# A linear-attention and SoLU feed-forward kernel: h multiplied by its exponential inside PSUM, three passes reading it there, two small negations on ScalarE, and a new order list

## The chip, the cores and the metric

The kernel runs on one core of a Trainium2 chip. The metric is the device time of one execution in microseconds (us). TensorE (PE) multiplies matrices, with a sequencer that also loads weights (PEld). VectorE (DVE), ScalarE (ACT) and GpSimd (POOL) do elementwise work, and SyncE (SP) issues the DMAs. Matrix products land in PSUM, which DVE and ACT can read and write here; everything else lives in SBUF.

## The reference

Inputs are q, k and v of shape 8 x 8 x 576 x 64 (batch, heads, sequence, head dimension), a weight of 512 x 1024, a weight of 1024 x 512 and a gain of 1024.

```python
q_s = softmax(q over the head dimension)          # exp(q - max) / (sum + 1e-9)
k_s = softmax(k over the sequence)
kv  = einsum('bhsd,bhse->bhde', k_s, v)
x   = einsum('bhsd,bhde->bhse', q_s, kv)          # then laid out as 4608 x 512
h   = x @ w_in                                    # 4608 x 1024
sm  = exp(h - max(h)) / (sum + 1e-9)              # per row
solu = h * sm
mu, var = mean and variance of solu per row
ln  = (solu - mu) / sqrt(var + 1e-6) * g_ln
out = ln @ w_out                                  # 4608 x 512
```

## The kernel before, in words

The 4608 rows are cut into 36 row tiles of 128 rows: four per batch, named b_c (batch 0 to 7, piece 0 to 3), and one more for each pair of batches that holds the last 64 rows of both (1_4, 3_4, 5_4, 7_4). The weights arrive as 64-bit floats in pairs of 32-bit words. They are rebuilt as 32-bit floats (lines 238 to 244; tiles iw and gw), scaled, and split into a high and a low fp16 part (lines 269, 271, 310 and 312; tiles wi and wo). Every matrix product of the feed-forward part is the sum of three fp16 products: high by high, high by low, low by high.

Each batch first has its keys (K) and queries (Q) put through the softmax: differences, exponentials, sums and products over 128 x 1024 pieces (lines 347 to 365 and 414 to 432), on DVE, ACT and POOL. For a row tile, `attend` (x) gives x transposed in two fp16 parts (xT, lines 505 and 507). `hidden` (h) does the following:

- 24 matmuls of 512 columns (line 522) into a PSUM tile h of 128 x 1024 fp32 (two of the 2-KB banks). There are two such tiles (tag "h", bufs=2), so the h of one tile has to wait until the tile two places earlier has let its buffer go.
- the negated row maximum (`top`, DVE, line 529), and `nm`, that times a scale (line 531).
- the exponential of h into an SBUF tile e, with its row sum (ACT, line 535).
- a chain of numbers per row, am, pi, p and ph (lines 539 to 548, POOL or DVE), which turns the maximum into a safe scale.
- s1: h times ph times e, written over e in SBUF, with its row sum (DVE, line 551). This is the last pass that reads h. Then `nmu`, the negated mean (line 553).
- u: the high fp16 part of e + nmu (ACT, line 556) and the low part (DVE, line 558); a DMA transposes both into uT (line 561). There are twelve uT buffers, so the h of many tiles can run ahead of their o.
- s2: the sum of squares of e + nmu (ACT, line 565), and another chain of numbers to r (POOL or DVE, lines 569 to 578).

`project` (o) multiplies uT by wo in 24 steps (line 593), into the only PSUM tile of tag "o", scales it by a number per row (line 601 on DVE or 603 on ACT) and stores it.

Each engine runs its instructions strictly in the order in which the program issues them. That order is written by hand: ORDER is a list of names; each name runs one more step of that piece of work (h5, o3, K2, Q2a, V21 and so on), up to its next `yield`. The letters after a dot (.v) put a step on DVE that would go to POOL or ACT. P is a step of four warm-up matmuls of TensorE, LK, LQ, LV, LG are loads, W and Z scale the two weights, w and y are the rebuilding of them.

Of the kernel before, what the change touches and what calls it, by code (L numbers as in the profile page):

```python
# [8 lines left out]
F32 = mybir.dt.float32  # L9
# [75 lines left out]
)  # L85


@with_exitstack
def linear_attention_solu_ffn(ctx: ExitStack, tc: tile.TileContext, q, k, v, w_in, w_out, g_ln, out):

# [420 lines left out]
    def hidden(row_tile):  # L511
# [50 lines left out]
        uT_of[row_tile] = uT  # L562
        yield
        s2 = sm.tile([P, 1], F32, name=f"s2{name}", tag="s2")
        nc.scalar.activation(e, e, AF.Square, bias=nmu, accum_out=s2)  # L565
        yield

        z1 = sm.tile([P, 1], F32, name=f"z1{name}", tag="z1")
# [144 lines left out]
```

## Time and profile before

| quantity | us |
|---|---|
| median of three runs | 516.03 |
| lowest and highest run | 513.93, 517.16 |
| the profiled execution | 514.96 |
| its span, first to last instruction | 513.1 |
| PE busy | 461.9 |
| DVE busy | 400.3 |
| ACT busy | 261.8 |
| POOL busy | 237.2 |

An engine's busy time is the time in which at least one of its instructions ran. Matmuls overlap one another, so a PE that is busy is not a PE at its peak. The profiled execution is 1.9 us longer than its span, and 1.1 us below the median of the runs.

### The profile page before, as it was taken

To read this page: it belongs to the slowest core of one execution; us is meant where nothing else is said; L and a number is where in the kernel's file an instruction comes from. 1 tells how busy PE (TensorE), PEld (TensorE's weight loads), DVE (VectorE), ACT (ScalarE), POOL (GpSimd) and SP (SyncE) were. 2 spreads that over 40 slices of the span, in tenths; PEclk is the share of its full clock that TensorE was granted. 3 is DMA by queue.
4 is the path that set the end of the run, shared out by engine and by line. 5 is a ranking of instruction groups with operands and counts; after the bars stand their busy time and mean duration, and the time that the engine had idled before them with its cause. 6 is when DMAs were issued, how large, how long until landed. Compare 5 with 4: busy or idle time off the path is not lost.

```text
span 513.1 us, 7978 instructions
## 1 busy us (share of the span) xinstructions
PE 461.9 (90%) x2986; PEld 234.5 (46%) x2986; DVE 400.3 (78%) x674; ACT 261.8 (51%) x378; POOL 237.2 (46%) x316
## 2 busy tenths in 40 slices
PE   4075796899989999999999999999999999999986
PEld 1043443444455444555554545544554544444434
DVE  4999999999989998989878896968876443455431
ACT  2466557876563644674446656444556423533430
POOL 5424686553884762937464367432552221202320
PEclk9578887999999999999999999999999999999999
DMA  7789649683778699758944866966072542252251
GB/s 268 204 243 257 144 135 205 158 163 98 118 186 202 154 182 221 143 101 231 210 98 118 222 134 158 203 173 131 14 144 64 122 77 69 61 125 61 61 144 41
DMA packets 159238, 74.97 MB, mean 146 GB/s; under 512 B 127840, under 2 KB 152672, under 8 KB 159200
## 3 DMA queue, kind: packets, MB, share of 16 engines
q1 hardware_dynamic: 159200, 74.47, 62.8%
q8 instruction: 23, 0.38, 0.3%
q14 instruction: 15, 0.12, 0.1%
HBM read 36.70 MB, written 9.44 MB: 90 GB/s over the span
## 4 chain that ended last, share of the span: by engine, by line
PE 44%; DVE 38%; POOL 5%; DMA 4%; issue 4%; ACT 3%; SPq 1%; DVEq 0%; POOLq 0%; ACTq 0%
PE o L593 22%; PE h L522 18%; DVE e L551 3%; DVE top L529 3%; DVE u L558 3%; DVE qsum L421 3%; DVE vm L150 2%; DMA w_in<-in_moe_w_in_dram 2%; DVE khalf L347 2%; DVE wi L271 1%; DMA qm<-in_q_dram 1%; DVE qnmx L414 1%; PE kv L375 1%; DVE wo L312 1%; POOL km L358 1%
## 5 line engine op out<-in xcount | busy, mean ns | idle before, releaser
L522 PE MATMUL h<-wi,xT 128*128 128x512 f16 x864 | 204.9, 384 | 7.4 <-DVE e L551 4.9
L593 PE MATMUL o<-wo,uT 128*128 128x512 f16 (+1 forms) x888 | 199.2, 373 | 3.8 <-DVE os L601 3.2
L593 PEld LDWEIGHTS <-uT 128*128 128x128 f16 x888 | 86.0, 98 | 99.9 <-issue 5.2
L522 PEld LDWEIGHTS <-xT 128*128 128x128 f16 x864 | 83.5, 99 | 105.5 <-issue 6.1
L529 DVE TENSOR_REDUCE top<-h 128x1 f32<-128x1024 f32 x36 | 43.8, 1216 | 38.7 <-PE h L522 38.6
L535 ACT ACTIVATE e<-h,nm,hs 128x1024 f32<-128x1024 f32 x32 | 38.4, 1201 | 49.8 <-DVE nm L531 38.5
L556 ACT ACTIVATE u<-e,nmu 128x1024 f16<-128x1024 f32 x36 | 41.1, 1146 | 38.3 <-DVE nmu L553 38.2
L558 DVE SCALAR_TENSOR_TENSOR u<-e,nmu,u 128x1024 f16<-128x1024 f32 x36 | 53.6, 1490 | 8.3 <-ACT u L556 8.2
L551 DVE SCALAR_TENSOR_TENSOR e<-h,ph,e 128x1024 f32<-128x1024 f32 x36 | 45.9, 1274 | 4.5 <-POOL ph L548 3.5
L539 POOL TENSOR_SCALAR am<-nm 128x1 f32<-128x1 f32 x22 | 12.7, 577 | 77.7 <-DVE nm L531 66.0
L565 ACT ACTIVATE e<-e,nmu 128x1024 f32<-128x1024 f32 x36 | 41.1, 1142 | 14.3 <-DVE u L558 14.3
L416 POOL TENSOR_TENSOR qm<-qm,qnmx 128x1024 f32<-128x1024 f32 (+1 forms) x13 | 26.6, 2050 | 29.0 <-DVE qnmx L414 29.0
L545 POOL TENSOR_TENSOR p<-pi,mone 128x1 f32<-128x1 f32 x36 | 21.6, 599 | 35.1 <-DVE pi L542 33.7
L427 POOL TENSOR_TENSOR qm<-qm,qrec 128x1024 f32<-128x1024 f32 (+1 forms) x13 | 26.7, 2056 | 20.0 <-DVE qrec L425 15.5
L432 POOL TENSOR_TENSOR qhl<-qm,qhl 128x1024 f16<-128x1024 f32 (+1 forms) x12 | 25.9, 2162 | 16.8 <-ACT qhl L148 12.5
L505 ACT ACTIVATE xT<-x 128x512 f16<-128x512 f32 x36 | 20.8, 589 | 24.1 <-PE h L522 14.3
L603 ACT ACTIVATE os<-o,rr 128x512 f32<-128x512 f32 x23 | 15.7, 683 | 29.5 <-PE o L593 15.7
L375 PE MATMUL kv<-vm,km 128*64 128x65 f32 x512 | 22.1, 228 | 8.3 <-ACT vm L148 4.9
L418 ACT ACTIVATE qm<-qm 128x1024 f32<-128x1024 f32 (+1 forms) x17 | 16.9, 1000 | 22.1 <-POOL qm L416 15.9
L358 POOL TENSOR_TENSOR km<-km,kb 128x1024 f32<-128x1024 f32 x9 | 23.3, 2585 | 8.6 <-ACT kb L333 8.3
L507 DVE SCALAR_TENSOR_TENSOR xT<-x,xT 128x512 f16<-128x512 f32 x36 | 24.3, 681 | 3.4 <-ACT xT L505 3.3
L578 POOL TENSOR_TENSOR r<-var,mhalf 128x1 f32<-128x1 f32 x36 | 24.6, 684 | 4.8 <-DVE var L575 3.7
(136 smaller groups left out, 658.6 us busy)
## 6 DMA issues: line engine op xcount, KB each, us to landing
v<-in_v_dram SPq DMA_DIRECT2D x32, 256.0 KB, 3.6
out_dram<-os SPq DMA_DIRECT2D x31, 256.0 KB, 3.2
qm<-in_q_dram SPq DMA_DIRECT2D x7, 1024.0 KB, 6.4
km<-in_k_dram SPq DMA_DIRECT2D x7, 1024.0 KB, 6.3
w_in<-in_moe_w_in_dram SPq DMA_DIRECT2D x8, 512.0 KB, 6.9
w_out<-in_moe_w_out_dram SPq DMA_DIRECT2D x8, 512.0 KB, 5.5
out_dram<-os SPq DMA_DIRECT2D x10, 128.0 KB, 2.6
qm<-in_q_dram SPq DMA_DIRECT2D x2, 512.0 KB, 4.3
```

What stands on the lines that cost most here:

```text
L358: on(nc.gpsimd).tensor_tensor(km[:, hs], km[:, hs], wide, op=ALU.subtract)
L375: nc.tensor.matmul(o, km[:, h + i, c], vm[:, h + i, c], start=(c == 0), stop=False)
L416: on(nc.gpsimd).tensor_tensor(x, x, wide(nmx), op=ALU.add)
L427: on(nc.gpsimd).tensor_tensor(x, x, wide(rec), op=ALU.mult)
L522: nc.tensor.matmul(h[:, ns], xT[:, t, kc], wi[:, s, kc, ns], start=(i == 0), stop=(i == len(terms) - 1))
L529: nc.vector.tensor_reduce(top, h, axis=AX.X, op=ALU.max, negate=True)
L535: nc.scalar.activation(e, h, AF.Exp, bias=nm, scale=hs, accum_out=z)
L551: nc.vector.scalar_tensor_tensor(e, h, ph, e, op0=ALU.mult, op1=ALU.mult, accum_out=s1)
L556: nc.scalar.activation(u[:, 0], e, AF.Identity, bias=nmu)
L558: nc.vector.scalar_tensor_tensor(u[:, 1], e, nmu, u[:, 0], op0=ALU.add, op1=ALU.subtract)
L565: nc.scalar.activation(e, e, AF.Square, bias=nmu, accum_out=s2)
L593: nc.tensor.matmul(o, uT[:, j, f], wo[:, s, f, cols], start=(f == 0 and j == 0 and s == 0), stop=(f == NF - 1 and j == 1))
```

## The change: what it does, and the diff

1. s1 (line 551) writes its product over h in PSUM and no longer over e in SBUF. The three passes behind it read it from h: u high (line 556, ACT), u low (line 558, DVE) and s2 (line 565, ACT). s2 leaves its unused squares in e. In the program as built, the first matmul into an h buffer now waits for ACT (for s2 of the tile two places earlier), where before it waited for DVE (for s1). s2 still stands behind u low, as before.
2. nm (line 531) and nmu (line 553), 36 of each, go from DVE to ACT.
3. The warm-up matmuls write into the PSUM tile of tag "o" (bufs=1) and no longer into that of tag "h".
4. ORDER is another list. DVE has 578 rows and had 635; ACT has 374 and had 293. Apart from nm and nmu, some steps change engine. DVE has 12 of the key differences (line 358) for 7, 7 of the query differences (line 416) for 4, and 6 of the query products (line 427) for 4. It has 9 of the copies of v (line 150) for 14. POOL has 4 key differences for 9, 10 query differences for 13 and 11 query products for 13.

```diff
 ORDER = (
-    "LQ0*2 w0 Q0a Q0a.v LK0 w0 Q0b Q0a*2 Q0c w0 K0 w1 Q0a LK0 w0 Q0a K0 Q0b*2 w0*2 w1 V02 w2 Q0c Q0b "
...
+    "LK0*3 w3 K0*2 w3 V00 LQ0 K0*3 P*4 K0*3 LQ0 w0*2 K0 w3 V00 K0.v LV0 w3 K0 w3 K0.v w3 K0*2 Q0a Q0b w0 "
...
 )
@@ hidden
         nm = sm.tile([P, 1], F32, name=f"nm{name}", tag="nm")
-        nc.vector.tensor_scalar(nm, top, hs, None, op0=ALU.mult)
+        nc.scalar.activation(nm, top, AF.Copy, scale=hs)
...
-        nc.vector.scalar_tensor_tensor(e, h, ph, e, op0=ALU.mult, op1=ALU.mult, accum_out=s1)
+        nc.vector.scalar_tensor_tensor(h, h, ph, e, op0=ALU.mult, op1=ALU.mult, accum_out=s1)
         nmu = sm.tile([P, 1], F32, name=f"nmu{name}", tag="nmu")
-        nc.vector.tensor_scalar(nmu, s1, -1.0 / DF, None, op0=ALU.mult)
+        nc.scalar.activation(nmu, s1, AF.Copy, scale=-1.0 / DF)
...
-        nc.scalar.activation(u[:, 0], e, AF.Identity, bias=nmu)
-        yield
-        nc.vector.scalar_tensor_tensor(u[:, 1], e, nmu, u[:, 0], op0=ALU.add, op1=ALU.subtract)
+        nc.scalar.activation(u[:, 0], h, AF.Identity, bias=nmu)
+        yield
+        nc.vector.scalar_tensor_tensor(u[:, 1], h, nmu, u[:, 0], op0=ALU.add, op1=ALU.subtract)
...
-        nc.scalar.activation(e, e, AF.Square, bias=nmu, accum_out=s2)
+        nc.scalar.activation(e, h, AF.Square, bias=nmu, accum_out=s2)
@@ warm_up
-            acc = ps.tile([P, DF], F32, name=f"warm_up{len(warmed)}", tag="h", bufs=2)[:, 0:DM]
+            acc = ps.tile([P, DM], F32, name=f"warm_up{len(warmed)}", tag="o", bufs=1)
```

The first place is DVE in the first row tiles. In the kernel before, from s1 of tile 0_1 on (L529 is top, L551 s1, L558 u low, the gw rows rebuild the second weight):

```order
L551 SCALAR_TENSOR_TENSOR e0_1_534,s10_1_569<-h0_1_462,ph0_1_553,e0_1_534 128x1024
L553 TENSOR_SCALAR nmu0_1_571<-s10_1_569 128x1
L244 SCALAR_TENSOR_TENSOR gw0_524<-w_out0_313,gw0_524 128x1024
L242 SCALAR_TENSOR_TENSOR gw3_530<-w_out3_374,gw3_530 128x1024
L529 TENSOR_REDUCE top0_0_597<-h0_0_511 128x1
L531 TENSOR_SCALAR nm0_0_599<-top0_0_597,hs0_484 128x1
L244 SCALAR_TENSOR_TENSOR gw3_530<-w_out3_374,gw3_530 128x1024
L558 SCALAR_TENSOR_TENSOR u0_1_609<-e0_1_534,nmu0_1_571,u0_1_609 128x1024
L529 TENSOR_REDUCE top0_3_684<-h0_3_585 128x1
```

And in the changed kernel, from s1 of its first tile, 0_0, on:

```order
L551 SCALAR_TENSOR_TENSOR h0_0_408,s10_0_535<-h0_0_408,ph0_0_529,e0_0_481 128x1024
L507 SCALAR_TENSOR_TENSOR xT0_2_525<-x0_2_468,xT0_2_525 128x512
L358 TENSOR_TENSOR km1_299<-km1_299,kb1_533 128x1024
L558 SCALAR_TENSOR_TENSOR u0_0_542<-h0_0_408,nmu0_0_537,u0_0_542 128x1024
L242 SCALAR_TENSOR_TENSOR gw0_441<-w_out0_380,gw0_441 128x1024
L244 SCALAR_TENSOR_TENSOR gw0_441<-w_out0_380,gw0_441 128x1024
L529 TENSOR_REDUCE top0_1_586<-h0_1_449 128x1
```

Between s1 and u low there were six instructions, the top of the next tile among them; now there are two, and the next top stands behind u low.

The second place is ACT in the same tiles. In the kernel before, from u high of tile 0_1 on (L535 is the exponential, L556 u high, L565 s2):

```order
L556 ACTIVATE u0_1_609<-e0_1_534,nmu0_1_571 128x1024
L148 COPY vm_76<-v1_3_550 128x8x64
L360 ACTIVATE km1_350<-km1_350 128x1024
L535 ACTIVATE e0_0_626,z0_0_627<-h0_0_511,nm0_0_599,hs0_484 128x1024
L148 COPY vm_76<-v1_2_582 128x8x64
L238 ACTIVATE gw1_654<-w_out1_602 128x1024
L565 ACTIVATE e0_1_534,s20_1_688<-e0_1_534,nmu0_1_571 128x1024
```

In the changed kernel, from nm of tile 0_0 on:

```order
L531 ACTIVATE nm0_0_461<-top0_0_459,hs0_439 128x1
L535 ACTIVATE e0_0_481,z0_0_482<-h0_0_408,nm0_0_461,hs0_439 128x1024
L148 COPY vm_76<-v1_1_484 128x8x64
L505 ACTIVATE xT0_2_525<-x0_2_468 128x512
L333 COPY kb1_533<-wide1_520 128x512
L553 ACTIVATE nmu0_0_537<-s10_0_535 128x1
L505 ACTIVATE xT0_3_540<-x0_3_500 128x512
L556 ACTIVATE u0_0_542<-h0_0_408,nmu0_0_537 128x1024
L565 ACTIVATE e0_0_481,s20_0_567<-h0_0_408,nmu0_0_537 128x1024
```

s2 stood five instructions behind u high, with the exponential of the next tile between them; now it follows at once, and nm and nmu stand in ACT's row.

## Rows read from the trace of the kernel before

**Rows 1.** The page: busy time of each engine, and the span in 40 slices

```profile
PE 461.9 (90%) x2986; PEld 234.5 (46%) x2986; DVE 400.3 (78%) x674; ACT 261.8 (51%) x378; POOL 237.2 (46%) x316
PE   4075796899989999999999999999999999999986
DVE  4999999999989998989878896968876443455431
```

**Rows 2.** Stretches: us, busy (instructions) of each engine, PEclk, DMA share, GB/s

```profile
0.00:51.00 51.00, 22.33 (x145) 11.00 (x146) 41.88 (x63) 25.54 (x35) 21.66 (x19) 0.76 0.86 242
51.00:130.00 79.00, 69.79 (x446) 35.38 (x444) 77.13 (x117) 53.10 (x78) 47.30 (x57) 0.92 0.65 149
130.00:215.00 85.00, 79.69 (x556) 41.70 (x555) 79.84 (x128) 45.34 (x67) 54.83 (x58) 1.00 0.84 177
215.00:270.00 55.00, 54.21 (x446) 29.22 (x444) 48.01 (x87) 28.74 (x43) 30.29 (x39) 1.00 0.70 160
270.00:488.00 218.00, 217.36 (x1297) 107.01 (x1296) 147.34 (x272) 105.58 (x155) 80.17 (x136) 1.00 0.50 113
488.00:513.00 25.00, 18.49 (x107) 10.18 (x105) 6.14 (x11) 3.51 (x5) 2.98 (x9) 1.00 0.38 95
```

**Rows 3.** Groups by form: busy us, mean ns | idle before, who ended it

```profile
L558 DVE SCALAR_TENSOR_TENSOR u<-e,nmu,u 128x1024 f16<-128x1024 f32 x36 | 53.6, 1490 | 8.3 <-ACT u L556 8.2
L551 DVE SCALAR_TENSOR_TENSOR e<-h,ph,e 128x1024 f32<-128x1024 f32 x36 | 45.9, 1274 | 4.5 <-POOL ph L548 3.5 <-ACT e L535 0.2
L529 DVE TENSOR_REDUCE top<-h 128x1 f32<-128x1024 f32 x36 | 43.8, 1216 | 38.7 <-PE h L522 38.6
L556 ACT ACTIVATE u<-e,nmu 128x1024 f16<-128x1024 f32 x36 | 41.1, 1146 | 38.3 <-DVE nmu L553 38.2
L565 ACT ACTIVATE e<-e,nmu 128x1024 f32<-128x1024 f32 x36 | 41.1, 1142 | 14.3 <-DVE u L558 14.3
L507 DVE SCALAR_TENSOR_TENSOR xT<-x,xT 128x512 f16<-128x512 f32 x36 | 24.3, 681 | 3.4 <-ACT xT L505 3.3
L531 DVE TENSOR_SCALAR nm<-top,hs 128x1 f32<-128x1 f32 x32 | 6.9, 214 | 1.2
L553 DVE TENSOR_SCALAR nmu<-s 128x1 f32<-128x1 f32 x36 | 5.5, 153 | 1.3
```

**Rows 4.** Single lines: duration in ns, lowest/median/highest, first and last start

```profile
L558 DVE SCALAR_TENSOR_TENSOR u<-e,nmu,u x36: 1264/1281/3142, 77.8 to 493.9; 128x1024 f16<-128x1024 f32 x36
L551 DVE SCALAR_TENSOR_TENSOR e<-h,ph,e x36: 1192/1276/1286, 68.4 to 491.2; 128x1024 f32<-128x1024 f32 x36
L271 DVE SCALAR_TENSOR_TENSOR wi<-iw,s_in,wi x4: 1191/2012/2322, 47.0 to 57.0; 128x1024 f16<-128x1024 f32 x4
```

**Rows 5.** Instructions in order of time: start us, us; ACT at the start

```profile
2.01 0.20 ACT L137 ACTIVATE warm<-mhalf 128x1 f32<-128x1 f32 x1
```

**Rows 6.** Instructions in order of time, the last two row tiles

```profile
478.63 1.22 DVE L529 TENSOR_REDUCE top<-h 128x1 f32<-128x1024 f32 x1 [4.99 <-PE h L522]
...
481.55 1.28 DVE L551 SCALAR_TENSOR_TENSOR e<-h,ph,e 128x1024 f32<-128x1024 f32 x1 [0.19 <-ACT e L535]
...
491.20 1.28 DVE L551 SCALAR_TENSOR_TENSOR e<-h,ph,e 128x1024 f32<-128x1024 f32 x1
...
493.90 1.28 DVE L558 SCALAR_TENSOR_TENSOR u<-e,nmu,u 128x1024 f16<-128x1024 f32 x1 [1.22 <-ACT u L556]
...
495.22 1.15 ACT L565 ACTIVATE e<-e,nmu 128x1024 f32<-128x1024 f32 x1 [1.35 <-DVE u L558]
```

**Rows 7.** The chain of waits, pieces in order of time: start us, us, what

```profile
119.79 1.15 DVE top L529
...
126.03 1.29 DVE e L551 x2
...
306.87 5.18 PE o L593 x24
...
312.48 0.06 PE x L471
```

124 rows, old and new, of the table ORDER are left out of this document.

## The prediction

> **What bounds the kernel now.** I read the page first [rows 1]. PE is the busiest engine, but its row is full only from the middle of the span on, while DVE's row is full from the second slice to about the fifteenth. The stretches say it more exactly [rows 2]. From 51 to 130 us DVE runs 77.1 of 79 us and PE 69.8; from 270 to 488 us PE runs 217.4 of 218 and DVE only 147.3. So the first part is DVE's and the second PE's. In the first part the two are coupled: every h needs DVE passes, and PE's work behind any point cannot begin before they end.
>
> The useful sum is therefore: when DVE has done what one h buffer waits for, plus the PE work that stands behind that h in program order. PE takes 0.216 us for a step of 512 columns (24 steps in 5.18 us) and 0.06 for a small step of attention [rows 7]. For DVE I went through its order list and gave each instruction the lowest or typical undisturbed duration of its line, less 0.07 us, since the next one starts that much before the end of the one ahead: a top of 1.22 moves the chain on by 1.15 [rows 3, 7].
>
> First point, in the kernel before: the h of tile 1_4 waits for s1 of 1_2. DVE's undisturbed work up to there is 95.1 us. It ended at 127.3 (126.03 + 1.28) [rows 7, 4]. Idle time explains 11.0 of the difference (51 - 41.9 and 79 - 77.1) [rows 2]. The other 21.2 us are DVE passes that lasted longer than they must. The lines show who suffers: u low takes 1.26 to 3.14 us, wi 1.19 to 2.32; both read two tensors from SBUF. s1, which reads one of its two from PSUM, never takes over 1.29 [rows 4]. POOL has 19 large passes (lines 358 to 432) ahead of that point, so a POOL pass costs DVE 1.12 us.
>
> Behind the point PE has 672 steps of h and 822 of o, 322.7 us, and 41.1 of small matmuls: 363.8. Sum 491.1. The span is 513.1; the 22 us between are PE's later gaps (5.3 us from 130 to 215, 6.5 in the last stretch [rows 2]), further disturbed passes and the drain.
>
> **The change part by part.** nm and nmu leave DVE: 32 and 4 times 0.214 plus 36 times 0.153 are 13.2 us [rows 3]. ACT takes 72 instructions; the nearest row is its 128x1 activation of 0.20 us [rows 5], so 14.4 us on an engine busy for half the span [rows 1]. The chain of a tile keeps its length (0.20 for 0.21 and 0.15) unless ACT is just in a pass of some 1.1 us [rows 3], so 0 to 1.1 us for each of 72; I take 0.2, and DVE's other work ahead of s1 hides it in the early tiles.
>
> In return DVE gets work from POOL: 5 more key differences, 3 query differences and 2 query products of about 1.2 us each undisturbed, 12 us. Against that stand five copies of v fewer and some small numbers per row. DVE's total is about even; what counts is the work ahead of the two points below.
>
> u low reads one tensor from SBUF. If it then behaves as s1 and xT do, its mean of 1490 ns falls to about 1270 [rows 3, 4]: 8 us of DVE over 36 tiles, 2.2 of it in the first ten. u high and s2 from PSUM: u high and s2 last 1146 and 1142 from SBUF, and I take the same, as ACT has room.
>
> s1 writes to PSUM. No row shows DVE writing there. Below, it costs nothing new: 1274 ns, as now with its read from PSUM [rows 3]. Above, if reading and writing one bank took turns, every element would pay twice, and s1 would grow by (1274 - 681) / 512 x 1024 = 1.19 us. I take the lower end, since s1 and u low differ by 5 ns in the median although one reads PSUM and the other does not [rows 4].
>
> The h buffer is held longer. Before, s1 frees it; now s2 does. From the end of the matmuls to the end of s2 the shortest chain of the trace is 2.92 (top to s1) plus 5.17 (s1 to s2), 8.1 us [rows 6], where it was 4.2. **Here a rule speaks against the change.** The rows show that a pass from PSUM costs DVE no more than one from SBUF (1276 against 1281 ns) [rows 4], so only the hold can cost. The Trainium skill, PSUM — Partial Sum Buffer, Summary: rules for kernel authors, says to evacuate promptly because PSUM is tight, and its page VectorE: DVE Perf Modes, Rules for kernel authors, would copy h out first if many operations follow. By the first rule the sum would rise as the second rival below does; by the rows the copy of the second would save nothing per pass.
>
> The order list answers to the hold. Between the last h step of a tile and the first of the tile two later, PE now has 7.7 to 9.2 us of other work in the first three tiles, and 13 to 21 in most that follow; before it was mostly 6 to 15. Only three later places are under 10 (9.6, 7.8, 9.1). What the buffer allows is thus mostly covered by the o steps that are put between.
>
> Now the same sum for the changed kernel. First point: h of 1_0 waits for s2 of 0_3. DVE's undisturbed work up to u low of 0_3 is 85.6, idle as before 11.0, POOL has 11 large passes ahead, 12.3; s2 ends 1.2 after u low [rows 6]. That is 110.1. Behind it PE has 744 steps of h and 816 of o, 337.0, and 43.7 of small ones: 380.7. Sum 490.8, against 491.1: DVE is 17 us earlier, but PE has 17 us more left.
>
> Second point, the largest later sum of each. Before: h of 3_1 waits for s1 of 2_3, 148.3 + 11.0 + 34 POOL passes x 1.12 (38.1) = 197.4, and 298.2 behind: 495.6. After: h of 2_2 waits for s2 of 2_1, 151.1 + 11.0 + 24 x 1.12 (26.9) + 1.2 = 190.2, and 305.8 behind: 496.0. From this 2.2 come off for u low. To be added are DVE's waits inside a tile: s1 cannot start before 1.7 us after top, nor u low before 1.4 after s1 [rows 6]. DVE's new order leaves less than that between them in few early tiles: 0.4 us missing up to this point, 3.8 over fourteen tiles, where the old order missed 0.2. I add 1. So 494.8 against 495.6.
>
> Between these points the old kernel's sums lie within some 6 us of its largest from tile 0_2 to 4_3; the new one's lie 5 to 10 below their largest at most tiles behind 3_1. A flat line of near-ties adds more small waits, and I take 1 more off. The later stretch has the same PE work and PE is full there [rows 2]. The missing waits of DVE over all tiles, 24 us, fall mostly there, where DVE idles for 71 us. The warm-up matmuls and the four more of them cost nothing: PE waits for weights then.
>
> Total -2 us: 514.96 - 2 = 513.0. The profiled execution lies 1.1 below the median of the runs, so by medians it is -0.6%.
>
> **The rivals.** (1) Faster: POOL's passes stop hurting. Two-input passes of DVE meet fewer and shorter POOL passes, and u low, the worst sufferer, leaves that group. If a POOL pass costs DVE half of 1.12, the 24 passes ahead of the second point give back 13 us there (to 481.8), the 11 ahead of the first 6 (to 484.8). The larger of the two then sets the end, 10 lower, and the time is 503. For it: 21 us of the first 127 are such loss. Against it: the steps that moved to DVE, key and query differences, read two tensors from SBUF themselves. Beside it the Trainium skill, SBUF — State Buffer, Who interferes with whom, says that a DVE operation with two SBUF inputs and a GpSimd operation that reads SBUF block each other for the whole instruction; by that rule u low can no longer be blocked, which the 3.14 against 1.29 us of the rows supports.
>
> (2) Slower: the hold. Where PE's cover is under 12 us, in eleven of 34 places, DVE's in-order list and ACT's queue stretch the 8.1 us to 10 to 13. If PE waits 1 us in each, the time is 524, and this decides from the point at which the hold exceeds the cover in more than about five places at 1 us. For it: the shortest covers, 7.7 to 9.2, are no longer than the shortest hold. Against it: in the early tiles this wait is the one already counted in the sums.
>
> (3) Slower: s1's write into PSUM costs the 1.19 us. Ten or eleven s1 stand ahead of the second point: 12 to 13 us more, 526.
>
> (4) The change does not do what it says: the passes from PSUM and nm on ACT are in the order lists, so this can only mean that contention and hold both do nothing. That is the forecast.
>
> **How the numbers follow.** A measurement of this kernel can tell about 1%, 5.2 us, from no change: faster means below 510.9 and slower above 521.2. Forecast 0.42, rival 1 0.34, rival 2 0.17, rival 3 0.07. The range reaches past rival 1's 503 to 501 and to the upper rivals' 526; beyond it lie some 0.12 of rival 1 and 0.08 of rivals 2 and 3, as each of these spreads by several us. The likeliest case's own range is 509 to 519, by the spread of the two points' sums and the waits added. Faster 0.34, same 0.42, slower 0.24.
>
> **What would show it.** In the changed profile: u low near 1.27 us and never over 1.3; s1 near 1.28 (rival 3 if near 2.4); nm and nmu near 0.2 on ACT. The first stretch to 130 us should have DVE as full as now, and PE's idle time before h should name ACT (s2); over 8 us of it in all would be rival 2. DVE's two-input passes in the first 130 us show rival 1: the sum of what they last beyond their lowest, 21 us now, should be 12 at the first point, under 7 for rival 1. A first top earlier or later than now by over 4 us, from the new order of the loads, would upset the idle 11 us that I kept, and with it the whole sum one for one.

## The result, and the profile after

The changed kernel takes 510.97 us (median of five runs, 509.67 to 511.37), the kernel before 514.36 in the same rounds (513.93 to 517.16). The ratio is 0.9916 with a 95% interval of 0.9891 to 0.9941: 0.8% faster. Forecast were 513.0 and -0.6%. The span fell from 513.1 to 509.2 us.

Of the page, the busy times and two of the rows in 40 slices, which answer to [rows 1]:

```profile
PE 463.3 (91%) x2990; PEld 235.3 (46%) x2990; DVE 374.5 (74%) x618; ACT 279.7 (55%) x457; POOL 197.5 (39%) x293
PE   7357875999999999899999999999999999999986
DVE  3999999999898989778867777788765464342521
```

DVE and POOL have 26 and 40 us less to do, ACT 18 more. DVE is still full up to the fifteenth slice or so, and PE behind it. The stretches, with the columns of [rows 2]:

```profile
0.00:51.00 51.00, 30.26 (x170) 14.75 (x171) 41.84 (x68) 27.25 (x38) 12.62 (x14) 0.73 0.80 241
51.00:130.00 79.00, 65.97 (x459) 33.71 (x457) 75.93 (x108) 54.24 (x90) 46.95 (x55) 0.96 0.71 160
130.00:215.00 85.00, 83.14 (x564) 43.35 (x563) 76.40 (x131) 55.44 (x91) 42.35 (x53) 1.00 0.81 177
215.00:270.00 55.00, 55.00 (x380) 28.34 (x379) 41.53 (x73) 30.18 (x52) 23.13 (x37) 1.00 0.65 147
270.00:488.00 218.00, 213.59 (x1333) 106.30 (x1332) 136.12 (x235) 112.60 (x189) 70.40 (x128) 1.00 0.52 118
```

What is new stands in the last two: PE misses nothing from 215 to 270 us (0.8 before), but 4.4 us from 270 to 488 (0.6 before). The groups by form that answer to [rows 3], and those of nm and nmu, now on ACT:

```profile
L522 PE MATMUL h<-wi,xT 128*128 128x512 f16 x864 | 204.9, 384 | 9.5 <-ACT e L565 8.5 <-DVE wi L271 0.6 <-DVE xT L507 0.4
L558 DVE SCALAR_TENSOR_TENSOR u<-h,nmu,u 128x1024 f16<-128x1024 f32 x36 | 46.1, 1280 | 18.3 <-ACT u L556 18.2
L551 DVE SCALAR_TENSOR_TENSOR h<-h,ph,e 128x1024 f32<-128x1024 f32 x36 | 46.3, 1287 | 12.8 <-POOL ph L548 10.7 <-ACT e L535 1.0 <-ACT xT L505 0.4
L556 ACT ACTIVATE u<-h,nmu 128x1024 f16<-128x1024 f32 x36 | 40.0, 1111 | 0.9
L565 ACT ACTIVATE e<-h,nmu 128x1024 f32<-128x1024 f32 x36 | 40.0, 1112 | 19.0 <-DVE u L558 18.9
L531 ACT ACTIVATE nm<-top,hs 128x1 f32<-128x1 f32 x32 | 9.4, 294 | 55.6 <-DVE top L529 55.4
L553 ACT ACTIVATE nmu<-s 128x1 f32<-128x1 f32 x36 | 7.3, 202 | 52.7 <-DVE h L551 52.6
```

The first row is the one to remember: PE's idle time ahead of h is ended by s2 (L565) now, 8.5 us in all. Before, the same row read:

```profile
L522 PE MATMUL h<-wi,xT 128*128 128x512 f16 x864 | 204.9, 384 | 7.4 <-DVE e L551 4.9 <-DVE xT L507 2.3
```

The single lines, as in [rows 4]:

```profile
L558 DVE SCALAR_TENSOR_TENSOR u<-h,nmu,u x36: 1268/1283/1286, 64.2 to 483.5; 128x1024 f16<-128x1024 f32 x36
L551 DVE SCALAR_TENSOR_TENSOR h<-h,ph,e x36: 1207/1292/1294, 61.1 to 480.8; 128x1024 f32<-128x1024 f32 x36
L551 DVE DVE_READ_ACCUMULATOR h<-h,ph,e x36: 82/141/143, 62.3 to 482.0; 128x1 f32 x36
L529 DVE TENSOR_REDUCE top<-h x36: 1161/1220/1226, 57.6 to 474.9; 128x1 f32<-128x1024 f32 x36
```

No u low is over 1.29 us any more; the longest was 3.14. The first top starts at 57.6 us, where it started at 63.3.

### The profile page after: what moved, and what is told of

Its sections match the earlier page's. It is cut to its first block, busy times and chain, and to the rows that moved or that the text cites. A ratio compares the mean times of both kernels' runs of the same rounds, so it can differ in the third digit from the quotient of the medians.

```text
span 509.2 us, 7977 instructions
## 1 busy us (share of the span) xinstructions
PE 463.3 (91%) x2990; PEld 235.3 (46%) x2990; DVE 374.5 (74%) x618; ACT 279.7 (55%) x457; POOL 197.5 (39%) x293
## 4 chain that ended last, share of the span: by engine, by line
PE 59%; DVE 25%; issue 6%; ACT 4%; DMA 3%; POOL 1%; SPq 0%; DVEq 0%; POOLq 0%; ACTq 0%
PE o L593 29%; PE h L522 23%; DVE u L558 3%; PE kv L375 2%; DVE bd L397 2%; DMA w_out<-in_moe_w_out_dram 2%; DVE top L529 1%; DVE qsum L421 1%; DVE qnmx L414 1%; ACT u L556 1%; DMA kr<-in_k_dram 1%; DVE khalf L347 1%; DVE wo L312 1%; DVE iw L242 1%; PE kv L377 1%
## 5 line engine op out<-in xcount | busy, mean ns | idle before, releaser
L529 DVE TENSOR_REDUCE top<-h 128x1 f32<-128x1024 f32 x36 | 43.8, 1216 | 33.8 <-PE h L522 33.8
L558 DVE SCALAR_TENSOR_TENSOR u<-h,nmu,u 128x1024 f16<-128x1024 f32 x36 | 46.1, 1280 | 18.3 <-ACT u L556 18.2
L551 DVE SCALAR_TENSOR_TENSOR h<-h,ph,e 128x1024 f32<-128x1024 f32 x36 | 46.3, 1287 | 12.8 <-POOL ph L548 10.7
L565 ACT ACTIVATE e<-h,nmu 128x1024 f32<-128x1024 f32 x36 | 40.0, 1112 | 19.0 <-DVE u L558 18.9
L556 ACT ACTIVATE u<-h,nmu 128x1024 f16<-128x1024 f32 x36 | 40.0, 1111 | 0.9
L531 ACT ACTIVATE nm<-top,hs 128x1 f32<-128x1 f32 x32 | 9.4, 294 | 55.6 <-DVE top L529 55.4
L535 ACT ACTIVATE e<-h,nm,hs 128x1024 f32<-128x1024 f32 x32 | 38.5, 1203 | 0.8
L553 ACT ACTIVATE nmu<-s 128x1 f32<-128x1 f32 x36 | 7.3, 202 | 52.7 <-DVE h L551 52.6
L601 DVE TENSOR_SCALAR os<-o,rr 128x512 f32<-128x512 f32 (+1 forms) x16 | 11.4, 715 | 27.1 <-PE o L593 27.1
L427 POOL TENSOR_TENSOR qm<-qm,qrec 128x1024 f32<-128x1024 f32 x11 | 21.7, 1975 | 20.7 <-DVE qrec L425 14.3
L473 PE MATMUL x<-qT,bd 128*128 128x128 f16 x128 | 24.1, 225 | 4.2 <-DVE bd L397 4.2
L375 PEld LDWEIGHTS kv<-vm,km 128*64 128x64 f32 x512 | 19.0, 147 | 14.0 <-issue 4.6
```

What stands on the lines that cost most here:

```text
L375: nc.tensor.matmul(o, km[:, h + i, c], vm[:, h + i, c], start=(c == 0), stop=False)
L473: nc.tensor.matmul(acc, al, bh, start=False, stop=True)
L529: nc.vector.tensor_reduce(top, h, axis=AX.X, op=ALU.max, negate=True)
L535: nc.scalar.activation(e, h, AF.Exp, bias=nm, scale=hs, accum_out=z)
L551: nc.vector.scalar_tensor_tensor(h, h, ph, e, op0=ALU.mult, op1=ALU.mult, accum_out=s1)
L556: nc.scalar.activation(u[:, 0], h, AF.Identity, bias=nmu)
```

## The experiments

All are given as a ratio to the kernel before, in the rounds that they share with it, with its 95% interval. The changed kernel itself, run once more beside three of them, gave 0.9915 [0.9888, 0.9943]; 0.1% is 0.5 us.

> The changed kernel once more, so that it stands on the same chip and in the same rounds as the three runs beside it: 511 by every theory.

It took 510.38 us. Its profiled execution again has 8.5 us of PE waiting for s2, in the same six places.

**The list and the passes apart.** The change has four parts that need not go together: the list, the passes in PSUM, nm and nmu on ACT, and the warm-up matmuls in the tile of tag "o". order_only keeps the list alone, so its warm-up matmuls still write into an h tile; new_negate takes only the passes out of the changed kernel, and new_inplace only nm and nmu.

```diff
 order_only: the kernel before, with the new ORDER and nothing else
 new_negate: the changed kernel, with
-        nc.vector.scalar_tensor_tensor(h, h, ph, e, ... accum_out=s1)
+        nc.vector.scalar_tensor_tensor(e, h, ph, e, ... accum_out=s1)
         # and u high, u low and s2 read e
 new_inplace: the changed kernel, with
-        nc.scalar.activation(nm, top, AF.Copy, scale=hs)
+        nc.vector.tensor_scalar(nm, top, hs, None, op0=ALU.mult)
-        nc.scalar.activation(nmu, s1, AF.Copy, scale=-1.0 / DF)
+        nc.vector.tensor_scalar(nmu, s1, -1.0 / DF, None, op0=ALU.mult)
```

> The kernel before with the new order list alone: e stays in SBUF, nm and nmu stay on DVE. Theory A (order and passes each give a part: DVE's work ahead of an h buffer sets the early stages, and the hold of the PSUM buffer gives some of it back later): ahead of the h of 2_2 DVE has 9 times 0.37 us of nm and nmu and 9 times 0.21 of u low more than the changed kernel, 5.2 us, and PE's 8.5 us of waiting for s2 fall away, of which I count 3 on the path: 513. Theory B (the order alone makes the gain, the hold only costs): 506 to 509, below the changed kernel. Theory C (the passes make the gain, the order only makes room for the hold and is worse by itself): 518 or more, above the kernel before. First top near 58 us by A and B, as in the changed kernel, since the loads' order decides it.

> The changed kernel with the passes back in SBUF (s1 writes e, u high, u low and s2 read e), so that s1 frees the h buffer; nm and nmu stay on ACT. A: u low is again 1.49 us in the mean, 1.9 us ahead of the h of 2_2, and PE's 8.5 us of waiting for s2 go, of which 2 to 3 are on the path: 510 to 511. B: 506 to 508, the hold was pure cost. C: 515 or more, since the reads from SBUF are disturbed again.

> The changed kernel with nm and nmu back on DVE; the passes still read and write PSUM. A: DVE has 9 times 0.37 us more ahead of the h of 2_2, 3.3 us, less some 1 for ACT's queue: 513. B: 509 to 511, as ACT's 0.29 us for nm and its queue leave the chain of a tile. C: 511, no change. nm 0.21 and nmu 0.15 us on DVE by all.

| list | passes | nm, nmu | warm-up | median us | ratio to before |
|---|---|---|---|---|---|
| new | SBUF | DVE (order_only) | h | 518.0 | 1.0054 [1.0035, 1.0072] |
| new | SBUF | ACT (new_negate) | o | 515.72 | 1.0003 [0.9979, 1.0028] |
| new | PSUM | DVE (new_inplace) | o | 512.12 | 0.9947 [0.9926, 0.9968] |
| new | PSUM | ACT (the change) | o | 510.38 | 0.9915 [0.9888, 0.9943] |

Two of these comparisons change one part alone. From new_negate to the changed kernel, the passes in PSUM bring 0.9%; from new_inplace to it, nm and nmu on ACT bring 0.3%, which is within the intervals. Theory C is right on the passes, and my theory A missed by 5 us on order_only and on new_negate. new_inplace lies between A's 513 and C's 511.

order_only is 0.5% slower than the kernel before, although its first top starts as early (56.7 us) as in the changed kernel. This is not the price of the list alone. The new list has a warm-up step behind the first h steps, and in order_only it needs an h buffer. In order of time, first in order_only, then in the changed kernel:

```profile
61.98 1.89 PE L648 MATMUL warm_up<-bd 128*128 128x512 f16 x4 [4.97 <-DVE e L551]
```

```profile
57.65 1.03 PE L648 MATMUL warm_up<-bd 128*128 128x512 f16 x4
```

PE stands for 4.97 us until s1 of the first tile has let its buffer go. The u low of 0_3 starts at 112.26 us in order_only and at 107.17 in new_negate, where the warm-up writes into the o tile. So the differences between order_only and the rows below it (0.5% and 1.1%) contain this wait besides nm and nmu or the passes. No run has the list and the warm-up tile without the rest.

In order_only the u low has its long cases again, in this single line:

```profile
L558 DVE SCALAR_TENSOR_TENSOR u<-e,nmu,u x36: 1270/1284/3085, 67.0 to 490.4; 128x1024 f16<-128x1024 f32 x36
```

**nm and nmu under the old list.** Here only they are moved. (The passes in PSUM under the old list were not tried: there, in 33 of 34 places, the h two places on is issued ahead of the s2 that would have to free its buffer.)

```diff
 old_negate: the kernel before, with
-        nc.vector.tensor_scalar(nm, top, hs, None, op0=ALU.mult)
+        nc.scalar.activation(nm, top, AF.Copy, scale=hs)
         yield
         # and nmu likewise
 old_late: the kernel before, and after_late: the changed kernel, each with
         yield
+        nc.scalar.activation(nm, top, AF.Copy, scale=hs)
         # and nmu likewise behind its yield, just before u high
```

> The kernel before, in its own order, with nm and nmu on ACT alone. A: DVE has 7 to 9 times 0.37 us less ahead of its points, 2.6 to 3.3 us: 511 to 512. B: 514 to 518, since ACT's nm waits behind passes of 1.1 us in an order that was not made for it. C: 514.

It took 541.6 us, 1.0513 [1.0471, 1.0555]: 26 us slower, where no theory had more than 4. The groups of ACT's nm and of PE's o in old_negate:

```profile
L531 ACT ACTIVATE nm<-top,hs 128x1 f32<-128x1 f32 x32 | 9.4, 293 | 73.1 <-DVE top L529 73.1
L593 PE MATMUL o<-wo,uT 128*128 128x512 f16 x840 | 197.2, 384 | 14.3 <-ACT os L603 12.0 <-DVE os L601 1.7 <-DVE wo L312 0.6
```

ACT stands at nm for 73 us until top is done, and PE's o waits 12 us for ACT to clear the only o buffer. PE's wait is less than half of the 26 us; the rest was not followed step by step. Counted in the order lists and added up over the 36 tiles, 51 ACT instructions stand between nm and the exponential in the old order, and 100 between nmu and u high; under the new one it is 15 and 13. (The expectations below have 80 for the 100 and 13 for the 15. These are sums, not numbers per tile.) Hence the next two runs, which issue nm and nmu one step later:

> The kernel before with nm and nmu on ACT, as in old_negate, but nm issued just before the exponential and nmu just before u high, one step later than there, so that nothing stands between them in ACT's queue. Theory D (old_negate loses because other ACT work, 51 instructions behind nm and 80 behind nmu, stands in the queue behind an instruction that waits for DVE): the loss goes, and DVE has 13 us less: 511 to 514. Theory E (it loses because nm and nmu themselves come late behind ACT's passes of 1.1 us): nm and nmu stand later still, so 538 or more.

> The changed kernel with the same step: nm issued just before the exponential and nmu just before u high. In its order only 13 and 13 ACT instructions stand between them. D: no change or up to 1 us faster, 510 to 511. E: 512 or more.

old_late took 512.42 us, 0.9945 [0.9924, 0.9966]: theory D. The 26 us are gone, and some 3 us more, without a new list and with the passes still in SBUF. The interval overlaps that of the whole change. The same groups in old_late:

```profile
L532 ACT ACTIVATE nm<-top,hs 128x1 f32<-128x1 f32 x32 | 9.3, 290 | 38.4 <-DVE top L529 38.2
L593 PE MATMUL o<-wo,uT 128*128 128x512 f16 x840 | 194.0, 380 | 2.2 <-DVE os L601 1.7 <-ACT os L603 0.5
```

ACT's wait is halved and PE's for ACT is 0.5 us. after_late took 512.03 us, 0.9941 [0.9921, 0.9961], not the gain of up to 1 us that D allowed, and just at the 512 of theory E; but its interval overlaps that of the changed kernel, so it shows no difference, and E's 538 for old_late was 26 us off. The new list has little to free.

**The hold.**

```diff
 after_short: the changed kernel, with
-        nc.scalar.activation(e, h, AF.Square, bias=nmu, accum_out=s2)
+        nc.scalar.activation(e, u[:, 0], AF.Square, accum_out=s2)
```

> The changed kernel with s2 taken from u high in SBUF (square of u high, no shift) and not from h, so that u low frees the h buffer some 1.3 us sooner and s2 does not wait for u low. Theory F (the hold of the buffer costs time in the changed kernel): PE's 8.5 us of waiting for s2 shrink to under 5 of waiting for u low, and the time falls by 1.5 to 3 us, to 508 to 509.5. Theory G (the hold is off the path, since the new order list loses as much behind 270 us without it): within 0.7 us of the changed kernel.

It took 506.03 us, 0.9831 [0.9802, 0.9860], 4.4 us below the changed kernel and the fastest of all that keep the whole computation; s2 is then summed from the rounded u high. In after_short the groups are:

```profile
L522 PE MATMUL h<-wi,xT 128*128 128x512 f16 x864 | 205.1, 384 | 3.7 <-DVE u L558 2.0 <-DVE wi L271 1.1 <-DVE xT L507 0.4
L565 ACT ACTIVATE e<-u 128x1024 f32<-128x1024 f16 x36 | 37.9, 1053 | 0.4
```

PE waits 2.0 us for the buffer where it waited 8.5, and s2 no longer waits 19 us for u low. Theory F is right, and even its 3 us were too few. This run changes two things, though: the buffer goes earlier, and ACT no longer stands at s2. The pair nopool_neg and nopool_after, below, parts the two.

**Why the passes gain.** What is left is where the gain comes from that outweighs this hold.

```diff
 ulow_sbuf: the changed kernel, with
-        nc.vector.scalar_tensor_tensor(u[:, 1], h, nmu, u[:, 0], op0=ALU.add, op1=ALU.subtract)
+        nc.vector.scalar_tensor_tensor(u[:, 1], e, nmu, u[:, 0], op0=ALU.add, op1=ALU.subtract)
 nopool_neg (new_negate) and nopool_after (the changed kernel): on POOL alone, for example in line 358,
-            on(nc.gpsimd).tensor_tensor(km[:, hs], km[:, hs], wide, op=ALU.subtract)
+            the same on km[:, hs, 0:1, 0:1] and wide[:, :, 0:1, 0:1]
         # and lines 363, 416 and 427 likewise
```

ulow_sbuf leaves out the low part of the product (it takes that of the exponential), and the nopool runs leave out most of POOL's differences and products.

> The changed kernel with one operand of u low turned back to SBUF: it reads the exponential e, which still lies there, and not h (so u low's values are left wrong); s1 still writes h, u high and s2 read h, and s2 still frees the buffer. Theory H (in place gains because u low no longer reads two tensors from SBUF and so is no longer held up beside POOL): u low's mean goes back from 1.28 to 1.43 us or more, and the time rises by most of what in place gains beside its hold, 4 to 8 us: 515 to 519. Theory J (the gain comes from u high and s2 on ACT, 35 ns faster each, or from s1 writing to PSUM, so that others find SBUF free): within 1.5 us of the changed kernel.

ulow_sbuf took 518.67 us, 1.0072 [1.0049, 1.0094]: one operand of one pass is worth 1.6%, 8 us. Theory H. The mean of its u low is 1461 ns:

```profile
L558 DVE SCALAR_TENSOR_TENSOR u<-e,nmu,u 128x1024 f16<-128x1024 f32 x36 | 52.6, 1461 | 18.6 <-ACT u L556 18.5
```

Most of the 36 are as short as in the changed kernel; seven last from 1.5 to 2.7 us, and only one of these stands in the first 110 us. One place of the order in both kernels, DVE's u low of tile 2_2 beside POOL's query differences (in order of time: start us, us, engine); first ulow_sbuf:

```profile
203.94 4.74 POOL L416 TENSOR_TENSOR qm<-qm,qnmx 128x1024 f32<-128x1024 f32 x2 [0.96 <-DVE qnmx L414]
204.38 2.54 DVE L558 SCALAR_TENSOR_TENSOR u<-e,nmu,u 128x1024 f16<-128x1024 f32 x1
```

and the changed kernel:

```profile
200.40 3.76 POOL L416 TENSOR_TENSOR qm<-qm,qnmx 128x1024 f32<-128x1024 f32 x2 [0.96 <-DVE qnmx L414]
200.84 1.27 DVE L558 SCALAR_TENSOR_TENSOR u<-h,nmu,u 128x1024 f16<-128x1024 f32 x1
```

With both tensors in SBUF, u low lasts 1.27 us longer and the two POOL passes 0.98 us longer: each engine pays. The Trainium skill, SBUF — State Buffer, Who interferes with whom, has the same: a DVE instruction with two SBUF inputs contends with a GpSimd one that reads SBUF, one with a single SBUF input does not, unless it runs in a mode that uses two ports. These rows agree.

> new_negate (passes in SBUF, s1 frees h) with POOL's large subtractions and products of lines 358, 363, 416 and 427 shrunk to one column, so that the maximum is not taken off keys and queries and the sums not divided out; only line 432 stays large on POOL. H: with POOL mostly gone the two-SBUF passes are not held up, and without a hold this kernel is as fast as nopool_after or up to 4 us faster. J: it stays some 4 us slower than nopool_after, as new_negate is to the changed kernel. Both are below 508, since a POOL pass costs DVE time elsewhere too.

> The changed kernel with the same four lines of POOL shrunk to one column. H: 500 to 508, and no faster than nopool_neg, since u low has nothing left to gain and the hold stays. J: some 4 us faster than nopool_neg.

nopool_neg took 501.03 us, 0.9747 [0.9709, 0.9785], and nopool_after 505.71, 0.9823 [0.9785, 0.9861]. The order of the two is turned round: without these POOL passes, the kernel with its passes in SBUF is 4 us faster (by the ratios), and each of its six runs is below each of the four of the other. POOL is not silent: it is busy for 147.3 and 138.5 us, and a few u low of nopool_neg are still long (1374 ns in the mean). In both kernels ACT waits some 20 us for u low ahead of s2, so ACT's wait is not the difference; the buffer is. The 4 us agree with after_short: the hold is on the path. The groups of h, first in nopool_neg, then in nopool_after:

```profile
L522 PE MATMUL h<-wi,xT 128*128 128x512 f16 x864 | 205.1, 385 | 1.5 <-DVE wi L271 1.1 <-DVE xT L507 0.4
```

```profile
L522 PE MATMUL h<-wi,xT 128*128 128x512 f16 x864 | 205.1, 384 | 10.2 <-ACT e L565 8.5 <-DVE wi L271 0.8 <-ACT xT L505 0.4
```

The wait for s2 is 8.5 us without these POOL passes as with them.

**The steps moved from POOL to DVE.**

```diff
 after_keys: the changed kernel, with every K0.v to K7.v of ORDER written K0 to K7
```

> The changed kernel with its 12 large and 3 small key differences of DVE (lines 358, 363) back on POOL, in the same places of the order: the work that the new list moved from POOL, and more. Theory K (as the prediction priced it: a POOL pass costs DVE 1.12 us, a DVE pass 1.15, so where it runs is a draw): within 1.5 us of the changed kernel's 511. Theory L (POOL's 2.6 to 2.9 us for what DVE does in 1.22 make the keys late, and keys hold up attention and with it PE): 514 or more. Theory M (POOL's cost to DVE is less, now that u low reads PSUM): 509 or less.

It took 516.33 us, 1.0012 [0.9995, 1.0029]: 5 us slower than the changed kernel, theory L. The key differences on POOL and the exponentials behind them, in after_keys:

```profile
L358 POOL TENSOR_TENSOR km<-km,kb 128x1024 f32<-128x1024 f32 x16 | 39.9, 2491 | 16.6 <-ACT kb L333 16.2
L360 ACT ACTIVATE km<-km 128x1024 f32<-128x1024 f32 x16 | 16.9, 1054 | 10.1 <-POOL km L358 10.1
```

In the changed kernel, 12 of the 16 are on DVE:

```profile
L358 DVE TENSOR_TENSOR km<-km,kb 128x1024 f32<-128x1024 f32 x12 | 14.7, 1228 | 2.4 <-ACT kb L333 2.3
L360 ACT ACTIVATE km<-km 128x1024 f32<-128x1024 f32 x16 | 16.8, 1052 | 0.8 <-DVE km L358 0.6
```

They take 1.23 us there, and the exponentials wait 0.8 us in place of 10.1. DVE's own load does not explain the loss: in after_keys DVE is busy for 367.2 us, 7.3 less than in the changed kernel. How the late exponentials reach PE was not followed.

## Why the prediction was right, point by point

**The bound and the first point: right.** I had h of 1_0 wait for s2 of 0_3, until 110.1 us. In the trace after, PE and ACT there:

```profile
109.91 1.02 PE L522 MATMUL h<-wi,xT 128*128 128x512 f16 x4 [0.78 <-ACT e L565]
108.66 1.11 ACT L565 ACTIVATE e<-h,nmu 128x1024 f32<-128x1024 f32 x1 [1.37 <-DVE u L558]
```

It began at 109.91. Before, h of 1_4 began at 128.05 (I had 127.3). With the PE work behind each, 380.7 and 363.8, the sums are 490.6 and 491.9: -1.2 us where I had -0.3. The two stretches of the trace after, cut at that point:

```profile
0.00:109.90 109.90, 76.15 (x468) 37.66 (x469) 98.71 (x152) 66.45 (x103) 47.17 (x50) 0.84 0.70 193
109.90:215.00 105.10, 103.23 (x722) 54.15 (x722) 95.47 (x154) 70.48 (x116) 54.75 (x72) 1.00 0.85 178
```

DVE's idle time ahead of it is 109.90 - 98.71 = 11.2 us; I had kept 11.0. The sign for rival 1 was not met there. Up to the end of u low of 0_3:

```profile
0.00:108.66 108.66, 75.67 (x467) 37.56 (x468) 97.47 (x150) 65.21 (x101) 45.95 (x49) 0.84 0.71 195
```

DVE is busy for 97.5 us, 11.9 more than the 85.6 of undisturbed work; the sum had 12.3, and rival 1 under 7. My sign for an upset, a first top more than 4 us off, did appear (5.7 us), but it was a bad sign: the idle time that it should have upset stayed at 11.2 us.

**The second point: wrong in its place.** I had h of 2_2 wait for s2 of 2_1, until about 189. It began at 187.49 with no idle time of PE ahead of it, while s2 of 2_1 ended only at 193.6: it took the buffer of 1_4, whose s2 ended at 186.1. "The tile two places earlier" is not a safe reading where tiles overtake one another. So of the 3.9 us of span, 1.2 came at the first point and 2.7 behind it, where I had put 1.7. The sum gave 2.0 us of 514.96, that is 0.4%; the -0.6% came from setting its 513.0, a profiled execution, against the median of other runs. Like for like, the profiled execution fell by 4.0 us, twice the sum.

**u low: the mechanism right, the term nearly four times too small.** 1280 ns for the 1270 I took, 7.5 us of busy time for 8. But I counted only the 2.2 us in the first ten tiles; ulow_sbuf says 8. The rest is what I had left to rival 1: u low also lengthens POOL's passes (POOL is busy for 209.3 us in ulow_sbuf and 197.5 in the changed kernel), and the loss falls late. The top of 0_3 starts at 98.0 us in ulow_sbuf and at 98.7 in the changed kernel's second run; that of 7_3 at 481.4 and 476.6. I had taken DVE's idle time in that part for a cover.

**The hold: right as a mechanism, mis-sized.** I let the sum carry 1.2 us at the second point and covered the rest. It costs some 4 us (4.4 in after_short, 3.9 between the two runs without POOL's passes). The sign of rival 2, over 8 us of PE waiting for s2, was met at 8.5; its 524 was not reached because the gain of u low is nearly twice as large. The Trainium skill, PSUM — Partial Sum Buffer, Summary: rules for kernel authors, says to evacuate promptly; here that is worth 0.8%, from one pass that need not read PSUM.

**s1 into PSUM: right.** 1287 ns for 1274, no sign of the 1.19 us of rival 3. The read-out of its sum takes 141 ns in the median, where it was 82, some 2 us over all tiles that I had not counted.

**nm and nmu: right in time, incomplete.** They bring 0.3% or 1.6 us in the new list, within the intervals, and 0.55% or 2.8 us in the old one if issued a step later (old_late); nine tiles of 0.37 us ahead of the second point would have been 3.3. I costed their own wait behind ACT's passes, and not what stands queued behind them: under the old list that is 26 us (old_negate). The new list avoids it; the sum came out without this step only because it was made from the new list.

**Work from POOL to DVE: wrong as a draw.** I set 1.12 us for a POOL pass against 1.15 for a DVE pass. after_keys shows 5 us for twelve large and three small ones: POOL takes 2.49 us for what DVE does in 1.23, and the exponentials wait.

**The warm-up matmuls: right only with the change's third part.** I had them cost nothing. In the changed kernel that holds; in an h tile the step among the first tiles makes PE wait 4.97 us (order_only).

So the forecast held in size in part by luck, because errors of both signs met: u low and the key differences were worth more than I gave them, and the hold cost more. What the list alone is worth stays open. With nm and nmu on ACT and the passes in SBUF, it is level with the kernel before (new_negate, 1.0003), where nm and nmu alone, issued a step later, gain 0.55% under the old list (old_late); but the two differ in that step too.

## What to carry to other kernels

Where DVE and POOL run side by side, look first for DVE passes with two SBUF tensors: taking one operand of one pass from PSUM was worth 8 us here, more than the 6.5 us by which DVE's own busy time for it differs. Then let the buffer go as early as the data allow, by giving the last reader another source. And before a small instruction goes to another engine, count what stands behind it in that queue until what it waits for is done; if that is much, issue it later.

## What the runs showed of the hardware that I had not expected

A 128x1 activation takes 294 ns with its scale from a tensor (nm) and 202 with a constant (nmu), where I took 200 for both. The Trainium skill, ScalarE: Activation LUTs, What ACT_TABLE_LOAD costs, gives some 93 ns for each such operand; the difference here, 92, agrees. ACT reads 128x1024 from PSUM in 1111 ns and from SBUF in 1146 [rows 3]. And an in-place pass of DVE in PSUM, reading and writing the same 128x1024, costs 13 ns more than one that writes to SBUF.
